# Normalised linear attention and a gated linear unit on one core: more buffers in four rings, and a new rotation of all of them, in an unchanged order

## The chip, the cores and the metric

The kernel runs on one core of a Trainium2 chip. The metric is the time of one execution on the device, in microseconds. PE is the matmul engine (TensorE), PEld its weight loads, DVE the vector engine, ACT the scalar engine, POOL is GpSimd, and SP the engine whose queue issues most DMAs. A name like L838 is line 838 of the kernel's file; the file has the same number of lines before and after the change, so a line number means the same in both.

## What is computed

Eight batches of eight heads, 576 positions, 64 values a head, in float32. The second half calls the first one's result `x`, with the heads side by side (512 columns).

```python
kv = np.einsum('bhsd,bhse->bhde', k, v)
out = np.einsum('bhsd,bhde->bhse', q, kv)
rms = np.sqrt(np.mean(out * out, axis=-1, keepdims=True) + 1e-06)
x = out / rms * g_norm            # then (B, H, S, D) -> (B, S, H*D)
...
for k in range(K):                # K = 5, a causal convolution along the positions
    gate_pre += conv_w[k][None, None, :] * xp[:, k:k + S, :]
gate = 1.0 / (1.0 + np.exp(-gate_pre))
val = x @ w_val
return (gate * val @ w_out).astype(np.float32)
```

The inputs `moe_w_val`, `moe_conv_w` and `moe_w_out` are of type float64; the kernel narrows them itself.

## The kernel before

**A list of steps.** The whole program is one string, `PLAN`, of 1242 steps in the order in which they are issued. Each step names a small function and its arguments (batch, chunk or column block, part), and after an `@` the buffers that its new data go to. An engine executes its own instructions strictly in the order of the list; between engines, and between an instruction and a DMA, a step waits by semaphores for whatever wrote its inputs, and for whatever last read or wrote the buffer that it takes. These waits follow from the list's order and from the buffers named in it. A PSUM bank counts as one buffer, even where a step uses half of it.

**Buffers.** `ROOMS` (L275) says how many buffers there are of each kind and how long one is; `new` (L283) hands out the one that the plan names:

```python
ROOMS = {"w64": (3, 1024), "ot": (3, 512), "wexp": (2, 512), "gate": (3, 576), "xs": (4, 576), "x": (2,
         512), "qT": (2, 2304), "k0": (1, 1152), "k1": (1, 1152), "v0": (1, 1152), "v1": (1, 1152), "ss": (2,
         36), "rt": (2, 36), "sq": (2, 520)}
...
rooms["bank"] = [psum.tile([P, 512], FP32, name=f"bank{n}") for n in range(8)]
...
room = rooms[tag][picked.pop(0)]
```

**The steps of a batch, in the order of the data.**
- `load_half`, `load_q` (L348, L358): DMAs of k, v and q from SP's queue. `turn_q` (L500, L503): DVE transposes q.
- `kv_product` (L476): PE makes k'v in two banks, 64 x 64 at a time; `kv_copy` (L490): ACT copies it out.
- `raw_pair`, `raw_tail` (L551): PE multiplies q by it, two chunks of 128 positions (or the last 64) into two banks. `square` (L600): ACT squares them into an `sq` buffer; `sums` (L607): DVE adds up; `powers` (L617): POOL takes the power -1/2; `normalise` (L636): ACT scales the raw product into an `x` buffer.
- `turn_blocks` (L661): DVE transposes `x` in blocks of 32; `move_blocks` (L669): DMAs from SP's and POOL's queues bring the blocks to their places in `xT`. The last chunk goes through PE instead (`turn_x`, L648; `keep_x`, L655). `halo` (L676): POOL.
- `gate_start` (L680): ACT begins a `gate` buffer; `gate_tap` (L686): DVE adds four taps; `gate_end` (L693): ACT's sigmoid.
- `x_sums` (L732), `val_fast` (L747), `val_keep` (L754 to L768): the product with `w_val` in seven half products instead of eight (Strassen's scheme), with sums of inputs made by DVE and sums of outputs put together by ACT copies and DVE adds. In a bank that goes on accumulating, the next half product waits until the copy in between has been taken. (`val_product`, L698, is the plain form for the first two batches.)
- `gated` (L711): DVE multiplies value and gate; this is the last reader of a `gate` buffer.
- `token_sums` (L816), `fast_product` (L838), `fast_keep` (L848 to L861): the product with `w_out`, two batches at a time, by the same scheme. `fast_product` uses one bank for `a`, and one bank for both `b` and `c`. `fast_keep` copies or adds into two `ot` buffers; `out_product` (L785) and `keep_out` (L793) do the last 64 positions plainly.
- `store` (L870): four DMAs of an `ot` buffer to the output, from SP's queue; `store_last`, from two queues, at the end.

At the start `narrow_weight` (L400 to L426) turns float64 weights into float32 with DVE and ACT; it takes `ot` and `wexp` buffers as scratch, and `start_warm` (L464) runs a few matmuls without use of their results.

The two functions that name the bank of half products and the copy of one half of it:

```python
elif bank != "a" and ("c", i, p) not in st:
    both = ps([P, 2, C // 2], f"cb{i}_{p}")
    st["b", i, p], st["c", i, p] = both[:, 0], both[:, 1]
...
elif n == 1:
    nc.scalar.copy(out=second[:, HIGH], in_=c)     # L852, fast_keep i p 1
```

Of the kernel before, what the change touches and what calls it, by code (L numbers as in the profile page):

```python
# [21 lines left out]
stage_weight cw 0 @ 0; turn_q_rows 0 1 @ 1; turn_q_rows 0 4 @ 0; sort_q 0 1 @ 0; turn_q_rows 0 0 @ 2;  # L22
sort_q 0 4; turn_q_rows 0 3 @ 3; turn_q_rows 0 2 @ 4; sort_q 0 0; start_warm 3 256 @ 0; load_q_rows 1 1;
load_q_rows 1 0; narrow_weight cw 0 0 @ 0; narrow_weight cw 0 5 @ 0; narrow_weight cw 0 1; sort_q 0 2;
stage_weight wval 3; kv_product 0 0 @ 1 2; narrow_weight cw 0 2; load_half k 1 0; narrow_weight cw 0 3;
load_half v 1 0; start_warm 1 256 @ 0; narrow_weight cw 0 6 @ 1; narrow_weight cw 0 4; kv_half 0 0;
narrow_weight cw 0 7; sort_q 0 3; turn_cw @ 4; kv_product 0 1; keep_cw; load_half k 1 1; stage_weight wval 2;
raw_half 0 3 0 @ 3; narrow_weight wval 1 5 @ 1; kv_half 0 1; load_half v 1 1; narrow_weight wval 1 0 @ 0;
raw_half 0 2 0 @ 4; narrow_weight wval 1 6 @ 0; narrow_weight wval 1 1; raw_half 0 3 1;
narrow_weight wval 0 5 @ 2; raw_half 0 2 1; stage_weight wout 1 @ 0; square 0 3 @ 0;  # L30
narrow_weight wval 0 6 @ 1; raw_half 0 4 0 @ 1; narrow_weight wval 1 2; sums 0 3 @ 0 0; raw_half 0 4 1;
square 0 2 @ 1; raw_half 0 0 0 @ 2; narrow_weight wval 0 0 @ 1; stage_weight wout 0 @ 1; powers 0 3;
square 0 4 @ 0; raw_half 0 0 1; sums 0 2; narrow_weight wval 1 3; raw_half 0 1 0 @ 0; sums 0 4; square 0 0 @ 1;
raw_half 0 1 1; narrow_weight wval 1 4; turn_q_rows 1 2 @ 5; load_q 2 2; square 0 1 @ 0; sums 0 0; powers 0 2;
narrow_weight wval 0 1; narrow_weight wval 1 7; turn_q_rows 1 0 @ 6; narrow_weight wval 0 2; sums 0 1;
turn_q_rows 1 3 @ 7; sort_q 1 2 @ 0; normalise 0 3 @ 0; narrow_weight wval 0 3; narrow_weight wval 3 5 @ 0;
turn_x 0 3 @ 5; powers 0 1; narrow_weight wval 3 6 @ 2; sort_q 1 0; turn_q_rows 1 1 @ 3; sort_q 1 3;
narrow_weight wval 3 0 @ 0; normalise 0 2 @ 0; narrow_weight wval 3 1; turn_q_rows 1 4 @ 7; normalise 0 4 @ 1;
turn_x 0 2 @ 4; keep_x 0 3; narrow_weight wval 0 4; narrow_weight wval 3 2; turn_x 0 4 @ 1;
kv_product 1 0 @ 6 5; narrow_weight wval 0 7; keep_x 0 4; narrow_weight wval 3 3; normalise 0 1 @ 1; halo 0;  # L40
keep_x 0 2; normalise 0 0 @ 0; stage_weight wout 2 @ 2; turn_x 0 1 @ 1; narrow_weight wval 3 4; turn_x 0 0 @ 2;
keep_x 0 1; narrow_weight wval 2 5 @ 1; val_product 0 1 1 @ 4; load_half k 2 0 @ 0; keep_x 0 0;
narrow_weight wval 3 7; narrow_weight wval 2 0 @ 1; gate_start 0 1 @ 0; narrow_weight wval 2 6 @ 2;
load_half v 2 1 @ 0; gate_start 0 0 @ 1; gate_tap 0 1 3; kv_product 1 1; gate_start 0 3 @ 2; gate_tap 0 0 3;
load_q 2 0; sort_q 1 1; val_product 0 3 1 @ 2; gate_tap 0 3 3; sort_q 1 4; kv_copy 1 0; kv_copy 1 1;
narrow_weight wval 2 1; narrow_weight wout 1 0 @ 0; narrow_weight wout 1 5 @ 1; gate_tap 0 0 2;
narrow_weight wval 2 2; raw_tail 1 @ 6 5; gate_tap 0 3 2; narrow_weight wval 2 3; raw_pair 1 3 @ 7 3;
square 1 4 @ 0; narrow_weight wout 1 6 @ 0; narrow_weight wout 1 1; val_product 0 1 0 @ 1; sums 1 4 @ 0 0;
square 1 3 @ 1; narrow_weight wval 2 4; powers 1 4; load_half v 2 0 @ 0; narrow_weight wout 1 2;
gate_tap 0 0 1; load_q 2 1; narrow_weight wout 1 3; sums 1 3; val_product 0 0 1 @ 0; keep_val 0 3 1;  # L50
narrow_weight wval 2 7; powers 1 3; square 1 2 @ 1; narrow_weight wout 1 4; normalise 1 4 @ 0; sums 1 2;
val_product 0 0 0 @ 2; val_sums 0; powers 1 2; normalise 1 3 @ 1; gate_tap 0 3 1; gate_tap 0 0 0;
val_product 0 2 0 @ 5; gate_tap 0 1 2; gate_end 0 0; gate_tap 0 3 0; keep_val 0 1 1; keep_val 0 0 0;
keep_val 0 0 1; narrow_weight wout 0 0 @ 1; raw_pair 1 1 @ 4 6; keep_val 0 1 0; narrow_weight wout 1 7;
narrow_weight wout 0 1; gated 0 0; turn_x 1 3 @ 1; square 1 0 @ 1; gate_tap 0 1 1; turn_x 1 4 @ 0;
val_product 0 2 1 @ 2; normalise 1 2 @ 1; sums 1 0; turn_q 2 0 @ 0; powers 1 0; gate_start 0 2 @ 1;
narrow_weight wout 0 5 @ 0; turn_x 1 2 @ 3; load_q 2 3; narrow_weight wout 2 5 @ 2; square 1 1 @ 1;
val_product 0 3 0 @ 7; narrow_weight wout 2 0 @ 0; gate_tap 0 2 3; keep_x 1 4; keep_x 1 3; keep_x 1 2;
gate_tap 0 2 2; load_half k 2 1 @ 0; narrow_weight wout 0 2; stage_weight wout 3 @ 0; kv_product 2 0 @ 3 1;
gate_tap 0 2 1; narrow_weight wout 0 3; sums 1 1; keep_val 0 2 0; val_product 1 0 1 @ 0; keep_val 0 3 0;  # L60
narrow_weight wout 0 4; keep_val 0 2 1; powers 1 1; gate_end 0 3; narrow_weight wout 0 6 @ 1;
normalise 1 0 @ 1; gate_tap 0 1 0; val_product 1 1 1 @ 2; narrow_weight wout 2 6 @ 0; halo 1; turn_q 2 2;
normalise 1 1 @ 0; narrow_weight wout 0 7; kv_product 2 1; gate_tap 0 2 0; keep_val 1 0 1; gate_end 0 1;
val_sums 1; turn_x 1 0 @ 0; gate_end 0 2; turn_q 2 1; turn_x 1 1 @ 4; keep_x 1 0; val_product 1 3 1 @ 6;
gated 0 3; load_q 3 0; narrow_weight wout 2 1; gated 0 2; kv_copy 2 1; keep_x 1 1; turn_q 2 3;
gate_start 1 1 @ 2; val_product 1 1 0 @ 4; load_q 3 1; weight_sums 0; kv_copy 2 0; keep_val 1 1 1; val_sums 2;
narrow_weight wout 2 2; gate_tap 1 1 3; keep_val 1 3 1; narrow_weight wout 2 3; raw_pair 2 3 @ 2 3;
load_half v 3 0 @ 0; narrow_weight wout 3 0 @ 1; load_half v 3 1 @ 0; narrow_weight wout 3 5 @ 1;
gate_tap 1 1 2; raw_pair 2 1 @ 1 6; square 2 2 @ 1; gated 0 1; square 2 3 @ 0; val_product 1 0 0 @ 0;
# [5 lines left out]
normalise 2 2 @ 1; sums 2 1; token_sums 0 0 2 @ 2; powers 2 1; square 2 0 @ 1; turn_blocks 2 3;
fast_product 0 0 0 @ 0; load_half k 3 1 @ 0; gate_start 1 3 @ 1; turn_q 3 1; fast_product 0 1 0 @ 2;
fast_keep 0 0 0 @ 0; weight_sums 1; keep_val 1 2 0; normalise 2 1 @ 0; fast_product 0 0 1 @ 3; sums 2 0;
gate_tap 1 0 3; raw_tail 2 @ 5 4; powers 2 0; fast_product 0 0 2; fast_keep 0 0 1 @ 2; weight_sums 2;
token_sums 0 0 3; fast_product 0 0 3; fast_keep 0 0 2; square 2 4 @ 1; turn_blocks 2 2; keep_val 1 2 1;
fast_product 0 0 5; fast_keep 0 1 0 @ 1; turn_blocks 2 1; normalise 2 0 @ 1; fast_product 0 0 4; sums 2 4;  # L80
fast_keep 0 0 5; powers 2 4; fast_product 0 1 2; gate_tap 1 0 2; store 0 0; kv_product 3 0 @ 6 1;
turn_blocks 2 0; fast_keep 0 1 2; normalise 2 4 @ 0; fast_keep 0 0 4; move_blocks 2 0; turn_q 3 2;
fast_product 0 1 4; gate_tap 1 0 1; move_blocks 2 2; turn_x 2 4 @ 4; fast_product 0 1 1 @ 5; gate_tap 1 0 0;
keep_x 2 4; move_blocks 2 1; kv_product 3 1; weight_sums 3; turn_q 3 3; move_blocks 2 3; fast_product 0 0 6;
gate_tap 1 3 3; kv_copy 3 0; kv_copy 3 1; gate_end 1 0; load_half v 4 0 @ 0; raw_pair 3 3 @ 1 6; load_q 4 0;
gate_tap 1 3 2; fast_keep 0 1 1 @ 0; gated 1 0; raw_pair 3 1 @ 3 4; fast_keep 0 1 4; square 3 3 @ 1;
gate_tap 1 1 1; fast_keep 0 0 6; fast_product 0 1 3; sums 3 3 @ 0 1; square 3 1 @ 0; load_half k 4 0 @ 0;
# [143 lines left out]
def kernel(  # L231
# [683 lines left out]
```

## Time and profile before

| | |
|---|---|
| time, median of 3 runs | 306.85 us (304.8 to 308.93) |
| the profiled execution | 305.46 us |
| its span, first to last instruction | 303.6 us |
| mean granted clock of PE | 0.995 |
| instructions | 8765 |

The span is what the profile's times refer to; 1.86 us lie around it. The page of the profile gives each engine's busy time, views by window give it by stage, and the timeline gives each instruction with the idle time of its engine ahead of it and what ended that time. PE's rows come in pairs for a float32 matmul of the program: "x4" at L838 is one half product of two matmuls.

### The profile page before, as it was taken

The numbers are of one execution on the slowest core, as the hardware profiler recorded it, in microseconds if no ns is written. First come the engines' busy times: TensorE is split into PE (matmuls) and PEld (weight loads), VectorE is DVE, ScalarE is ACT, GpSimd is POOL, SyncE is SP. The second block draws the span as 40 slices with busy tenths as digits, with TensorE's granted clock in tenths as the row PEclk, the third lists the DMA queues.
The fourth block names the chain that finished last, engine by engine and source line by source line (L and its number), as shares of the span: only waits on it lengthen the run. The fifth ranks groups of instructions, "written<-read, shape, count | busy, mean of one in ns | idle before, by whom it ended". The sixth has DMA issues, their size and how long they took to land.

```text
span 303.6 us, 8765 instructions
## 1 busy us (share of the span) xinstructions
PE 292.6 (96%) x3333; PEld 226.0 (74%) x3333; DVE 273.0 (90%) x482; ACT 194.5 (64%) x606; POOL 112.5 (37%) x127
## 2 busy tenths in 40 slices
PE   7989999999999989999999999999999999999993
PEld 3778777788786765877878757787877588788582
DVE  1899999999998999999999999999999999999612
ACT  2998989989567654983586537682878354434220
POOL 3072355045647046165327552245635731000000
PEclk9999999999999999999999999999999999999997
DMA  7999976578479466978688587928411721112423
GB/s 270 378 385 367 302 189 215 146 231 250 122 190 333 123 186 143 316 200 241 177 238 284 135 220 192 328 53 225 104 37 42 169 69 35 37 43 63 104 69 104
DMA packets 32073, 55.51 MB, mean 183 GB/s; under 512 B 6166, under 2 KB 14358, under 8 KB 32032
## 3 DMA queue, kind: packets, MB, share of 16 engines
q1 hardware_dynamic: 29520, 49.76, 55.8%
q0 software_dynamic: 1632, 3.17, 4.4%
q10 hardware_dynamic: 880, 2.03, 1.9%
q8 instruction: 26, 0.43, 0.6%
q14 instruction: 15, 0.12, 0.1%
HBM read 39.21 MB, written 9.44 MB: 160 GB/s over the span
## 4 chain that ended last, share of the span: by engine, by line
PE 70%; DMA 12%; DVE 9%; SPq 4%; issue 2%; ACT 1%; DVEq 0%; ACTq 0%
PE bank L838 29%; PE bank L747 23%; DMA qs<-in_q_dram 9%; PE bank L785 5%; PE bank L698 4%; PE bank L551 4%; DVE gate L686 3%; PE bank L476 3%; DMA k<-in_k_dram 2%; SPq L669 2%; DMA out_dram<-ot 2%; PE bank L648 1%; SPq L358 1%; PE bank L521 1%; PE bank L515 1%
## 5 line engine op out<-in xcount | busy, mean ns | idle before, releaser
L617 POOL TENSOR_TENSOR rt<-ss,mhalf 128x8 f32<-128x8 f32 (+3 forms) x38 | 68.0, 1794 | 100.3 <-DVE ss L607 100.3
L686 DVE SCALAR_TENSOR_TENSOR gate<-xT,cwT,gate 128x576 f32<-128x576 f32 x128 | 101.7, 812 | 2.3 <-ACT gate L680 0.8
L636 ACT ACTIVATE x<-bank,rt 128x64 f32<-128x64 f32 x252 | 55.8, 359 | 6.3 <-POOL rt L617 4.1
L838 PE MATMUL bank<-wsum,w 128*128 128x256 f32 x192 | 48.9, 385 | 0.9 <-ACT ot L850 0.6
L838 PEld LDWEIGHTS bank<-wsum,w 128*128 128x128 f32 x192 | 35.4, 190 | 8.8 <-DVE w L816 1.1
L747 PE MATMUL bank<-xs,vsum 128*128 128x288 f32 x144 | 38.1, 408 | 0.0
L669 POOL DMA_DIRECT2D xT<-y x48 | 26.4, 557 | 27.2 <-ACT ot L852 13.7
L838 PE MATMUL bank<-wout,gv 128*128 128x256 f32 x128 | 33.0, 384 | 0.3 <-ACT x L636 0.3
L698 PE MATMUL bank<-xT,wval 128*128 128x288 f32 x128 | 32.8, 409 | 0.0
L747 PEld LDWEIGHTS bank<-xs,vsum 128*128 128x128 f32 x144 | 27.1, 190 | 7.4 <-ACT x L636 0.4
L693 ACT ACTIVATE gate<-gate 128x576 f32<-128x576 f32 x32 | 22.2, 704 | 10.8 <-DVE gate L686 10.6
L848 DVE TENSOR_TENSOR ot<-bank,ot 128x512 f32<-128x512 f32 (+1 forms) x32 | 17.5, 547 | 12.4 <-PE bank L838 7.1
L698 PEld LDWEIGHTS bank<-xT,wval 128*128 128x128 f32 x128 | 23.7, 190 | 6.1
L600 ACT ACTIVATE sq<-bank 128x256 f32<-128x256 f32 (+1 forms) x70 | 21.9, 390 | 9.0 <-PE bank L551 8.6
L747 PE MATMUL bank<-xT,wval 128*128 128x288 f32 x96 | 26.8, 411 | 0.5 <-DMA out_dram<-ot 0.2
L838 PEld LDWEIGHTS bank<-wout,gv 128*128 128x128 f32 x128 | 23.8, 190 | 4.4 <-ACT x L636 0.5
L680 ACT ACTIVATE gate<-xT,cwT 128x576 f32<-128x576 f32 x32 | 25.0, 807 | 3.1 <-DVE gv L711 3.1
L607 DVE TENSOR_REDUCE ss<-sq 128x8 f32<-128x520 f32 (+1 forms) x40 | 24.9, 632 | 0.7 <-ACT sq L600 0.6
L711 DVE TENSOR_TENSOR gv<-gv,gate 128x576 f32<-128x576 f32 x32 | 23.6, 751 | 1.0 <-ACT gate L693 0.8
L747 PEld LDWEIGHTS bank<-xT,wval 128*128 128x128 f32 x96 | 17.7, 190 | 5.0 <-issue 0.7
L551 PEld LDWEIGHTS bank<-kv,qT 64*64 64x64 f32 x1008 | 16.4, 134 | 5.6 <-issue 2.4
L676 POOL COPY xT<-xT 128x124 f32<-128x124 f32 x32 | 16.0, 538 | 10.5 <-ACT xT L655 10.5
(93 smaller groups left out, 451.5 us busy)
## 6 DMA issues: line engine op xcount, KB each, us to landing
qs<-in_q_dram SPq DMA_DIRECT2D x96, 140.0 KB, 4.0
out_dram<-ot SPq DMA_DIRECT2D x140, 64.0 KB, 1.7
k<-in_k_dram SPq DMA_DIRECT2D x14, 576.0 KB, 6.0
v<-in_v_dram SPq DMA_DIRECT2D x12, 576.0 KB, 5.5
xT<-y SPq DMA_DIRECT2D x48, 64.0 KB, 2.9
xT<-y POOLq DMA_DIRECT2D x48, 64.0 KB, 3.2
y<-in_moe_w_val_dram SPq DMA_DIRECT2D x4, 512.0 KB, 11.6
w<-in_moe_w_out_dram SPq DMA_DIRECT2D x4, 512.0 KB, 10.0
```

The source lines that it names most:

```text
L551: nc.tensor.matmul(st["raw", b, c][r][cols, to * D:(to + 1) * D], st["qT", b][rows, hp, first:first + D], kvs[b % 2][rows, hp, :], start=T ...
L607: nc.vector.reduce_sum(out=st["ss", b][:, FIRST[c]:FIRST[c] + n], in_=st["sq", b, c][:, 0:n], axis=AX.X)
L617: nc.gpsimd.tensor_tensor(out=st["rt", b][:, which], in0=st["ss", b][:, which], in1=mhalf[:, which], op=ALU.pow)
L636: nc.scalar.activation(out=x[:, to * D:(to + 1) * D], in_=raw[:, h * D:(h + 1) * D], func=AF.Copy, scale=root[:, to:to + 1])
L669: (nc.sync if i % 2 else nc.gpsimd).dma_start(out=xTs[b % 2][i * TB:(i + 1) * TB, :, first:first + P], in_=y[a * TB:(a + 1) * TB, i])
L680: nc.scalar.activation(out=gate[:], in_=xTs[b % 2][:, jt, HALO:SX], func=AF.Copy, scale=cwT[:, K - 1, jt:jt + 1])
L686: nc.vector.scalar_tensor_tensor(out=gate[:], in0=xTs[b % 2][:, jt, tap * TB:tap * TB + S], scalar=cwT[:, tap, jt:jt + 1], in1=gate[:], op ...
L693: nc.scalar.activation(out=gate[:], in_=gate[:], func=AF.Sigmoid)
L698: nc.tensor.matmul(val[:], wval[:, kc, jt * P:(jt + 1) * P], xTs[b % 2][:, kc, HALO + n * SV:HALO + (n + 1) * SV], start=(kc == 0), stop=( ...
L711: nc.vector.tensor_tensor(out=both, in0=both, in1=st["gate", b, jt][:], op=ALU.mult)
L747: nc.tensor.matmul(st[bank, "val", b, mj][:], weights_[:, k], tokens()[:, k], start=(n in (0, 1, 3) and k == 0), stop=(k == NK // 2 - 1), ...
L838: nc.tensor.matmul(st[bank, i, p], tokens()[:, k], weights_[:, k], start=(n < 2 and k == 0), stop=(k == NK // 2 - 1), skip_group_check=True)
```

## The change

Four rings get one buffer more each: output buffers (`ot`) 3 to 4, gates 3 to 4, x chunks 2 to 3, buffers of squares 2 to 3. The number of PSUM banks stays at 8. In the plan, each step that takes a buffer now takes the one that has been free longest, in the enlarged rings as in the others and in the banks.

Each engine's and each DMA queue's instructions stand in the same order as before, one by one; the only new instruction is one memset of 128 x 8 (L325) for the third buffer of squares. The list interleaves the engines a little differently, which matters only where two steps of different engines share a buffer.

How far apart the takings of one buffer lie, counted in takings of its kind, from the two plans:

| kind | before: buffers, least, mean | after: buffers, least, mean |
|---|---|---|
| `ot` | 3, 1, 2.96 | 4, 2, 4.00 |
| `gate` | 3, 1, 3.00 | 4, 2, 4.00 |
| `x` | 2, 1, 1.95 | 3, 2, 2.97 |
| `sq` | 2, 1, 1.97 | 3, 2, 3.00 |
| `xs` | 4, 1, 3.45 | 4, 3, 4.00 |
| bank | 8, 1, 7.55 | 8, 1, 7.92 |

The diff, with a few of the plan's 209 lines:

```diff
-    ROOMS = {"w64": (3, 1024), "ot": (3, 512), "wexp": (2, 512), "gate": (3, 576), "xs": (4, 576), "x": (2,
+    ROOMS = {"w64": (3, 1024), "ot": (4, 512), "wexp": (2, 512), "gate": (4, 576), "xs": (4, 576), "x": (3,
              512), "qT": (2, 2304), "k0": (1, 1152), "k1": (1, 1152), "v0": (1, 1152), "v1": (1, 1152), "ss": (2,
-             36), "rt": (2, 36), "sq": (2, 520)}
+             36), "rt": (2, 36), "sq": (3, 520)}
...
-val_keep 2 0 2; gate_end 1 3; val_fast 2 1 1 @ 7; val_keep 2 1 2; gate_start 1 2 @ 2; val_fast 2 0 4;
+val_keep 2 1 2; gate_start 1 2 @ 0; load_q 4 1; val_fast 2 0 4; sums 3 0; val_keep 2 0 1; gated 1 1;
...
-kv_product 4 1; token_sums 0 1 0 @ 2; token_sums 0 1 2 @ 1; fast_keep 0 2 0 @ 1; raw_tail 3 @ 3 1;
+fast_keep 0 2 0 @ 2; load_q 4 2; raw_tail 3 @ 0 3; token_sums 0 1 2 @ 2; fast_product 0 3 0 @ 2;
...
-fast_product 2 2 1 @ 3; gate_tap 6 1 2; gated 6 2; val_fast 6 1 3 @ 0; val_keep 6 1 4; gate_start 6 0 @ 2;
-val_keep 6 1 5; fast_product 2 2 3; val_keep 6 1 3; normalise 7 4 @ 0; gate_tap 6 1 1; val_fast 7 1 0 @ 1;
-fast_keep 2 2 1 @ 0; token_sums 2 1 1; turn_x 7 4 @ 2; val_fast 7 1 3 @ 7; val_keep 7 1 0; token_sums 2 1 3;
+gate_tap 6 1 2; fast_product 2 2 1 @ 4; gate_start 6 0 @ 1; gated 6 2; val_fast 6 1 3 @ 5; normalise 7 4 @ 2;
+val_keep 6 1 4; fast_keep 2 2 1 @ 2; val_keep 6 1 5; fast_product 2 2 3; val_keep 6 1 3; gate_tap 6 1 1;
+val_fast 7 1 0 @ 2; token_sums 2 1 1; turn_x 7 4 @ 3; token_sums 2 1 3; val_keep 7 1 0; val_fast 7 1 3 @ 6;
```

More of the change, by code (lines that the diff above doesn't have):

```diff
@@ L75 @@
[L75 to L84, printed above, removed]
@@ new lines @@
+powers 2 2; keep_val 1 3 0; normalise 2 3 @ 1; narrow_weight wout 3 7; narrow_weight wout 2 4;
+load_half k 3 0 @ 0; load_q 3 2; val_product 1 2 0 @ 7; normalise 2 2 @ 0; narrow_weight wout 2 7; sums 2 1;
+token_sums 0 0 2 @ 1; powers 2 1; square 2 0 @ 2; fast_product 0 0 0 @ 5; turn_blocks 2 3; gate_start 1 3 @ 3;
+load_half k 3 1 @ 0; turn_q 3 1; fast_product 0 1 0 @ 1; fast_keep 0 0 0 @ 2; keep_val 1 2 0; weight_sums 1;
+normalise 2 1 @ 2; fast_product 0 0 1 @ 0; sums 2 0; raw_tail 2 @ 7 3; gate_tap 1 0 3; powers 2 0;
@@ new lines @@
+turn_blocks 3 1; fast_product 0 2 3; sums 3 4; move_blocks 3 1; fast_product 0 3 2; fast_keep 0 2 4;
+gate_tap 2 1 3; val_fast 2 0 3 @ 1; powers 3 4; move_blocks 3 3; fast_keep 0 3 2; turn_q 4 2; move_blocks 3 2;
+fast_product 0 3 1 @ 4; gate_tap 2 0 2; normalise 3 4 @ 2; move_blocks 3 0; fast_product 0 2 5; gate_tap 2 0 1;
+gate_start 2 3 @ 3; turn_q 4 3; fast_product 0 2 6; gate_tap 2 0 0; raw_pair 4 3 @ 0 6; gate_tap 2 1 2;
+out_product 0 8 @ 3; square 4 3 @ 0; fast_keep 0 2 5; fast_keep 0 2 6; gate_tap 2 3 3; store 0 4;
@@ new lines @@
+square 4 2 @ 1; gate_end 2 0; sums 4 3 @ 0 0; gate_tap 2 1 1; powers 4 3; gate_tap 2 3 2; load_half v 5 0 @ 0;
+turn_x 3 4 @ 5; sums 4 2; store 0 5; keep_x 3 4; gate_tap 2 1 0; powers 4 2; val_keep 2 0 3; gate_end 2 1;
+val_fast 3 0 0 @ 7; x_sums 3 0 @ 1; fast_keep 0 3 1 @ 1; normalise 4 3 @ 1; x_sums 3 1 @ 0; raw_pair 4 1 @ 1 5;
+load_half v 5 1 @ 0; gated 2 1; load_q 5 0; fast_product 0 3 3; val_keep 3 0 0; x_sums 3 3 @ 3;
+normalise 4 2 @ 0; turn_blocks 4 3; fast_product 0 3 4; gated 2 0; load_half k 5 0 @ 0; gate_start 2 2 @ 0;
@@ new lines @@
+val_fast 3 0 2; fast_keep 0 3 4; gate_tap 2 3 1; gate_start 3 2 @ 1; fast_product 0 3 5; square 4 1 @ 2;
+gate_tap 2 3 0; square 4 0 @ 0; val_fast 3 1 1 @ 0; turn_blocks 4 2; fast_keep 0 3 5; val_fast 3 1 0 @ 6;
+x_sums 3 2 @ 2; store 0 6; fast_product 0 3 6; val_keep 3 1 0; sums 4 0; gate_end 2 3; sums 4 1;
+val_fast 3 1 2; gated 2 3; load_q 5 1; powers 4 1; val_fast 3 0 1 @ 4; val_keep 3 1 2; gate_tap 2 2 3;
+val_keep 3 1 1; val_keep 3 0 2; val_fast 3 1 4; fast_keep 0 3 6; gate_tap 2 2 2; keep_out 0 8 @ 2; powers 4 0;
@@ new lines @@
+gated 2 2; kv_copy 5 1; val_fast 3 0 3 @ 0; fast_keep 1 0 0 @ 0; square 4 4 @ 1; token_sums 1 0 0 @ 0;
+kv_copy 5 0; store 0 7; move_blocks 4 0; token_sums 1 0 1; fast_product 1 0 1 @ 7; move_blocks 4 1;
+gate_tap 3 0 3; fast_product 1 0 2; move_blocks 4 3; gate_tap 3 0 2; val_fast 3 1 3 @ 3; fast_keep 1 0 2;
+sums 4 4; gate_start 3 3 @ 3; val_keep 3 1 4; powers 4 4; fast_keep 1 0 1 @ 3; gate_tap 3 0 1; val_fast 3 1 6;
+token_sums 1 0 3; normalise 4 4 @ 0; fast_product 1 0 4; turn_q 5 3; fast_product 1 0 3; turn_q 5 2;
@@ new lines @@
+powers 6 1; gate_start 5 2 @ 3; turn_blocks 6 2; fast_product 2 1 2; token_sums 2 0 3; fast_keep 2 0 2;
+square 6 0 @ 0; gate_tap 5 2 3; fast_product 2 0 5; fast_keep 2 1 2; normalise 6 1 @ 1; sums 6 0;
+fast_product 1 2 0 @ 1; token_sums 1 1 0 @ 1; powers 6 0; fast_product 2 0 4; fast_keep 2 0 5; turn_blocks 6 3;
+store 2 0; fast_product 2 1 4; fast_keep 2 0 4; normalise 6 0 @ 0; turn_q 7 0 @ 1; fast_product 2 1 1 @ 6;
+gate_tap 5 2 2; fast_product 2 0 6; load_q 7 3; turn_blocks 6 1; raw_tail 6 @ 2 7; fast_keep 2 0 6;
@@ new lines @@
+val_fast 6 1 2; halo 6; fast_keep 1 3 4; normalise 7 0 @ 2; gate_tap 5 1 0; fast_product 1 3 6; x_sums 6 2 @ 2;
+val_keep 6 1 2; val_fast 6 0 2; gated 5 0; sums 7 1; val_fast 6 1 1 @ 6; val_keep 6 0 2; turn_blocks 7 0;
+gate_end 5 1; powers 7 1; val_fast 6 1 4; turn_blocks 7 2; val_keep 6 0 1; fast_keep 1 3 6; val_keep 6 1 1;
+fast_keep 1 3 5; store 1 7; gate_end 5 3; val_fast 6 0 4; normalise 7 1 @ 1; gated 5 3; val_fast 6 1 5;
+gated 5 1; store 1 6; val_fast 6 0 3 @ 4; gate_start 6 3 @ 3; token_sums 2 1 2 @ 0; turn_blocks 7 1;
@@ L212 @@
 gate_tap 7 1 0; store 3 1; fast_product 2 3 5; gated 7 0; gate_end 7 1; fast_product 3 1 0 @ 3;
[L213 to L214 removed]
+fast_keep 2 3 5; gate_start 7 3 @ 3; gate_tap 7 2 2; val_fast 7 1 5; store 2 6; fast_keep 3 1 0 @ 1;
+fast_keep 2 3 4; val_fast 7 1 6; val_keep 7 1 5; gate_tap 7 3 3; fast_product 3 1 3; val_keep 7 1 6;
```

337 lines of the change are left out of this document (155 added, 182 removed).

## The prediction

> **What bounds the kernel now.** I read the page's busy times first, then the same by stage, then the chain of waits and the timeline of each engine where a stage shows a hole.
>
> ```profile
> PE 292.6 (96%) x3333; PEld 226.0 (74%) x3333; DVE 273.0 (90%) x482; ACT 194.5 (64%) x606; POOL 112.5 (37%) x127
> ```
>
> PE is the bound, and DVE is close behind. By stage (after the times come PE, PEld, DVE, ACT, POOL busy, the granted clock, the DMA share and GB/s):
>
> ```profile
> 94.00:111.00 17.00, 15.25 (x211) 11.65 (x210) 15.27 (x29) 11.10 (x40) 3.00 (x4) 1.00 0.69 213
> 111.00:264.00 153.00, 152.45 (x1585) 116.43 (x1584) 149.43 (x249) 94.66 (x313) 68.75 (x81) 1.00 0.59 163
> 264.00:287.00 23.00, 22.95 (x103) 16.94 (x101) 21.36 (x34) 8.81 (x20) 0.00 (x0) 1.00 0.26 66
> 300.00:303.60 3.60, 0.00 (x0) 0.00 (x0) 0.00 (x0) 0.00 (x0) 0.00 (x0) 0.58 0.35 93
> ```
>
> After the first 20 us, PE idles 1.75 us in one stage of 17 us and less than 0.6 us in each of the others up to 287; DVE idles 1.73 us there and 3.57 us from 111 to 264. A busy PE is not a PE at its peak, so I also need the step of its stream when nothing holds it. The chain gives it:
>
> ```profile
> 126.13 0.86 PE bank L838 x4
> 127.00 1.94 PE bank L747 x8
> ```
>
> Four instructions of an output product (L838) take 0.865 us, four of a value product (L747) 0.97. Against these steps I look for starts that come late. The one cluster is this, PE first, then ACT, then DVE (start, length, what, in brackets the idle time before it and its releaser):
>
> ```profile
> 96.64 2.21 PE L747 MATMUL bank<-xT,vsum 128*128 128x288 f32 x8 [0.65 <-ACT gv L758]
> 105.83 1.13 PE L838 MATMUL bank<-wout,gv 128*128 128x256 f32 x4 [0.34 <-ACT x L636]
> 107.56 1.13 PE L838 MATMUL bank<-wsum,w 128*128 128x256 f32 x4 [0.60 <-ACT ot L850]
> 108.85 1.99 PE L838 MATMUL bank<-wsum,w 128*128 128x256 f32 x8 [0.16 <-ACT gv L768]
> ```
>
> ```profile
> 95.53 0.77 ACT L680 ACTIVATE gate<-xT,cwT 128x576 f32<-128x576 f32 x1 [1.78 <-DVE gv L711]
> 99.37 1.75 ACT L636 ACTIVATE x<-bank,rt 128x64 f32<-128x64 f32 x8 [0.84 <-DVE y L661]
> 104.03 1.74 ACT L636 ACTIVATE x<-bank,rt 128x64 f32<-128x64 f32 x8 [0.33 <-DVE y L661]
> 107.13 0.37 ACT L850 COPY ot<-bank 128x256 f32<-128x256 f32 x1 [1.36 <-DMA out_dram<-ot]
> ```
>
> ```profile
> 96.34 1.67 DVE L686 SCALAR_TENSOR_TENSOR gate<-xT,cwT,gate 128x576 f32<-128x576 f32 x2 [0.84 <-ACT gate L680]
> 98.57 0.71 DVE L661 STREAM_TRANSPOSE y<-x 128x512 f32<-128x512 f32 x1 [0.19 <-ACT x L636]
> 106.06 0.68 DVE L816 TENSOR_TENSOR w<-w,gv 128x512 f32<-128x512 f32 x1
> 110.94 0.42 DVE L848 TENSOR_TENSOR ot<-bank,ot 128x256 f32<-128x256 f32 x1 [0.62 <-ACT gv L768]
> ```
>
> All four waits of ACT are waits for a buffer: a gate that is still multiplied (L711), an x chunk not yet transposed (L661, twice), an output buffer not yet stored. PE's late starts stand behind them: its releaser each time is a copy that was queued on ACT.
>
> **The change, part by part.** Every engine and every DMA queue issues the same instructions in the same order; only the buffers differ, and so the waits. One set-up memset is new; the two like it take 65 ns each, and DVE then idles 5.5 us for the first inputs: cost 0.
>
> *The cluster, 94 to 111.* With a fourth gate, gate_start runs when ACT is free, at 93.37 + 0.38 = 93.75 instead of 95.53, and the copy that frees PE (L758, next in the queue) ends near 94.8 instead of 96.59. PE's previous group starts at 94.86 and lasts 0.97, so PE starts at 95.83 instead of 96.64: 0.81. The third x chunk takes away 0.84 and 0.33, the fourth output buffer 1.36. PE's start at 105.83 could have been at 105.01 + 0.27 = 105.28 (16 small products of the group at 105.01): 0.55. The one at 107.56 could follow at 105.83 + 0.865 + 0.10 = 106.80 (after each wait the second step is 0.10 late, hence 1.13 above where four undisturbed take 1.03): 0.76. The one at 108.85, at 107.56 + 0.97 = 108.53: 0.32. Sum 2.44. But the product at 107.56 also needs DVE's sum, which ends at 106.06 + 0.68 = 106.74. DVE gains 0.84 + 0.19 = 1.03 by then, so it is there at 105.71 and PE cannot start before 105.76: 1.80 gained, not 2.12. With the 0.32 behind it, PE leads by **2.1 us** at 111 (bounds: 0.8 if only the gate matters, 2.44 if DVE holds nothing). DVE, whose 0.62 at 110.94 was a wait for PE, leads by 1.65.
>
> *From 111 to 264.* PE has 0.55 us idle left, so its lead can hardly grow: 0 (to 0.45, two starts at 181 and 222). DVE's lead grows by part of its 3.57 us: its waits for PE (0.52 and 0.21) by what PE leads beyond it, some 0.45, and a little of those for ACT; I take 0.6 of bounds 0 and 3.57, nearer the bottom since most of its idle time is the pipeline's own, under 0.15 us a time. DVE's lead is then 2.2. The other ACT waits that go in this stage (for stores 1.23 at 211.86; for gates 0.94 at 244.78) lie before copies for which PE does not wait.
>
> *One wait is new and late.* I laid the new buffers over the old times: 92 waits of PE are new, and 91 of them end before PE's old start or within 0.1 us of it. The other:
>
> ```profile
> 246.42 0.37 ACT L852 COPY ot<-bank 128x256 f32<-128x256 f32 x1
> 245.35 1.03 PE L838 MATMUL bank<-wout,gv 128*128 128x256 f32 x4
> ```
>
> The list now has the copy of half a bank (fast_keep 2 2 1) ahead of the product into its other half (fast_product 2 2 3); it was behind. So PE waits for ACT at 245.35. ACT no longer waits 0.94 for its gate there, so the copy starts at 245.48 and ends at 245.85: PE starts 0.55 late, and 0.10 for the next step. PE also loses what it leads beyond ACT, which follows DVE: 2.1 - 1.65 = 0.45. Cost **1.1** (bounds: 0 if ACT is well ahead; 246.79 - 245.35 = 1.44, + 0.16 = 1.6 beyond any lead if it isn't). Behind the waiting product stand value products and, through them, DVE's adds; DVE has other work in its queue.
>
> *From 264 on.* PE's starts at 263.35, 281.55 and 287.05 wait for DVE sums and adds and are 0.26, 0.31 and 0.20 late; DVE's lead of 2.2 covers them: **0.8** gained (0 if DVE gained nothing). ACT's store waits (0.84, 0.72) hide under a PE that is 22.95 of 23.00 us busy. The end (the last copy at 298.58, its four stores, 3.6 us without matmuls) is the same.
>
> *Before 94.* The waits that go here (for squares, x, narrowed weights) are on ACT and DVE, 0.2 to 0.3 us each; PE's late starts there are the first inputs, and 0.36 for a load of k. I take 0, up to 0.5.
>
> Sum: 2.1 - 1.1 + 0.8 = **1.8 us**. The profiled execution took 305.46 us (span 303.6, 1.86 around it), so 303.7; the median of the runs shown, 306.85, lies 1.39 above it, and on that footing I forecast **305.0 us**, 0.6% less. A measurement here can tell about 2% (6.1 us; the three runs spread over 4.1) from no change.
>
> One rule bears on how much could be open. The Trainium skill, "Perfetto Trace Analysis", section "Identifying the Most-Contended Engine", says to judge TensorE by the busy share of weight loads, not of matmuls. By it 74% counts, a quarter of the span is open, and a gap that recurs can mean too few buffers (section "Optimization Strategy"). Here a load takes 190 ns of a 216 ns step even in an unbroken stream, so 88% is its most in L838; the sum above does not use the rule, and D below is what it would make.
>
> **Rivals.**
> *B, no gain* (306.9): DVE, 97% busy from 20 to 264, is the true bound and its order is kept; PE's lead of 2.1 is spent in waits for DVE sums. For it: 107.56 is already held by DVE. Against: DVE's own 1.65 us in the cluster were waits, and they go.
> *C, slower* (308.5): the shared bank at 245. ACT is not early, PE loses 1.6 there, and nothing of the cluster stays, as DVE holds PE elsewhere: 305.46 + 1.6, + 1.39 for the median. It decides from the point where ACT's copy comes later than 245.3. Over 2% it would need four such places, and I find one.
> *D, much faster* (294): all of the weight loads' waits after 20 us that name an engine or a DMA are buffer waits. They add up to 12.8 us (longest 1.1): 306.85 - 12.8. Against: most are 0.3 to 0.4 us at changes of tile size and end under the matmuls still running.
> *E, slower by a clock* (319): rotating through more banks leaves PE short pauses, and the clock falls. The last stage above has 0.58 granted after 1.4 us without matmuls began it; a stage of 17 us at 0.58 would take 17/0.58 = 29.3, so 12.3 more. Against: 1.00 in every stage with work, the cluster's 1.75 us of idle included. The Trainium skill, "TensorE: Matmul & The Clock Gate", section "A second HAM failure mode: psum-queue depth-cycling", speaks for it: cycling through PSUM banks idled the PE often enough for its clock to swing. By that rule the cluster should show it before, and it doesn't.
> *The change does nothing*: excluded, as the late starts name buffers that become more.
>
> **How the numbers follow.** Forecast 0.68, B 0.13, C 0.09, D 0.07, E 0.03. The range is 301.5 to 308.2: from a gain of 4 us or so (every late start after 20 us, at a low run) to C with a run at its middle, with 1.5 us for the spread of the runs; it leaves out D, E and the ends. Over 2% faster is D, 0.07; over 2% slower E and 0.02 of C, 0.05; 0.88 between.
>
> **What would show it.** Right: PE's starts of the cluster undelayed, ACT without waits for L711, L661 or stores there, PE's idle from 94 to 111 below 0.5 us, a new wait of 0.4 to 1.5 us of PE for ACT's L852 near 243, and PE waits for L816 and L848 gone after 260. Wrong: new PE waits for ACT of over 1 us at more than one place, DVE idle unchanged at 5 us from 94 to 264, a clock under 1.00 before 300, or a span below 298 or above 306.

## The result, and the profile after

| | before | after |
|---|---|---|
| median time | 305.82 us (304.4 to 308.93, 21 runs) | 302.94 us (301.69 to 305.54, 21 runs) |
| ratio | | 0.9906 (95%: 0.988 to 0.9932) |
| the profiled execution, its span | 305.46, 303.6 us | 305.54, 303.8 us |

The change makes the kernel 2.9 us (0.94%) faster; forecast were 1.8 us and 305.0. The time lies in the range, and the direction is clear of the noise though the gain is small. The forecast stood on the median of three runs, 306.85; the median of 21 is 1.03 us lower, and that is half of the 2.06 us by which the time came out below 305.0. The other half is the gain, which was larger than forecast. The profiled execution happens to be the slowest of the 21 after the change, so its span must not be compared with the one before. It has to be read by stage; a second and a third profile of the same kernel (below) have spans of 301.6 and 300.2.

The busy times of the page are nearly those of before, with POOL's 5.0 us larger:

```profile
PE 290.7 (96%) x3333; PEld 225.8 (74%) x3333; DVE 272.6 (90%) x483; ACT 193.2 (64%) x606; POOL 117.5 (39%) x127
```

By stage, with the columns of the prediction's table:

```profile
20.00:94.00 74.00, 71.10 (x1152) 57.37 (x1149) 70.98 (x124) 61.74 (x187) 38.77 (x32) 1.00 0.78 223
94.00:111.00 17.00, 16.78 (x221) 13.56 (x220) 16.89 (x30) 13.02 (x48) 5.26 (x6) 1.00 0.84 253
111.00:264.00 153.00, 151.58 (x1583) 116.22 (x1582) 149.50 (x250) 93.57 (x312) 69.50 (x81) 1.00 0.61 164
264.00:287.00 23.00, 22.96 (x103) 17.57 (x104) 21.57 (x35) 9.08 (x21) 0.00 (x0) 1.00 0.24 61
300.00:303.80 3.80, 0.00 (x0) 0.00 (x0) 0.00 (x0) 0.00 (x0) 0.00 (x0) 0.78 0.47 132
```

From 94 to 111 PE idles 17.00 - 16.78 = 0.22 us where it idled 1.75, DVE 0.11 where it idled 1.73 (in this execution the same work comes 2.7 us later, so the two windows do not hold quite the same instructions; the table of stretches below does not have this fault). The new idle time is in the first row: 2.9 us of PE's 74. Here is its largest piece, in the timeline of POOL, ACT and PE:

```profile
37.46 10.79 POOL L617 TENSOR_TENSOR rt<-ss,mhalf 128x8 f32<-128x8 f32 x3 [0.55 <-DVE ss L607]
46.83 1.74 ACT L636 ACTIVATE x<-bank,rt 128x64 f32<-128x64 f32 x8 [1.99 <-POOL rt L617]
48.63 0.66 PE L648 MATMUL bank<-ident,x 128*128 128x128 f32 x4 [1.86 <-ACT x L636]
```

and the same place of POOL before the change:

```profile
36.80 4.61 POOL L617 TENSOR_TENSOR rt<-ss,mhalf 128x8 f32<-128x8 f32 x2 [0.55 <-DVE ss L607]
45.19 1.64 POOL L617 TENSOR_TENSOR rt<-ss,mhalf 128x8 f32<-128x8 f32 x1 [3.78 <-DVE ss L607]
```

In this one execution the second of the three powers, at 40.1, took 6.69 us where it took 1.96, and ACT and PE stood behind it. PE reaches the cluster at 96.62 instead of 93.89. In the cluster itself the waits have gone. PE first, then ACT:

```profile
106.90 1.13 PE L838 MATMUL bank<-wout,gv 128*128 128x256 f32 x4
108.25 2.83 PE L838 MATMUL bank<-wsum,w 128*128 128x256 f32 x12 [0.22 <-DVE w L816]
110.92 1.03 PE L838 MATMUL bank<-wout,gv 128*128 128x256 f32 x4
96.23 0.78 ACT L680 ACTIVATE gate<-xT,cwT 128x576 f32<-128x576 f32 x1
97.48 3.40 ACT L636 ACTIVATE x<-bank,rt 128x64 f32<-128x64 f32 x16
104.96 1.73 ACT L636 ACTIVATE x<-bank,rt 128x64 f32<-128x64 f32 x8
106.53 0.42 ACT L850 COPY ot<-bank 128x256 f32<-128x256 f32 x1
```

None of the four ACT rows has a wait: not the gate (1.78 before), not the two x chunks (0.84 and 0.33), not the output buffer (1.36). Of the three products at L838 that began late, the one of 105.83 now starts without a wait (106.90), and the other two are part of an unbroken 12; what is left is one wait for DVE's sum (0.22). And the new wait at 245 is there, one place, as the prediction laid it out (PE's weight load names the releaser):

```profile
245.84 0.39 ACT L852 COPY ot<-bank 128x256 f32<-128x256 f32 x1
246.28 0.73 PEld L838 LDWEIGHTS bank<-wout,gv 128*128 128x128 f32 x4 [0.57 <-ACT ot L852]
246.28 1.13 PE L838 MATMUL bank<-wout,gv 128*128 128x256 f32 x4
```

Since matmul number n is the same one in every profile, PE's lead over the profile of before can be taken at any mark. A stretch between two marks is free of what came earlier. This is where PE gained and lost in the three profiles of the changed kernel, in us (marks by the times of before):

| from, to | forecast | first | second | third |
|---|---|---|---|---|
| start to 93.9 | 0 | -2.73 | -0.71 | +0.62 |
| 93.9 to 112.4, the cluster | +2.1 | +2.50 | +2.50 | +2.40 |
| 112.4 to 244.4 | 0 | -0.41 | -0.29 | -0.08 |
| 244.4 to 246.2, the new wait | -1.1 | -0.39 | -0.38 | -0.39 |
| 246.2 to 297.7 | +0.8 | +0.38 | +0.37 | +0.37 |
| 297.7 to the end | 0 | +0.54 | +0.52 | +0.56 |

The last five rows add up to 2.6 to 2.9 us, which is the gain in the medians; the first row differs from run to run. All of this is measured against the one profile that was taken of the kernel before.

### The profile page after: what moved, and what is told of

Same layout as the page of the kernel before. It is cut to its first block, busy times and chain, and to the rows that moved or that the text cites. A ratio compares the mean times of both kernels' runs of the same rounds, so it can differ in the third digit from the quotient of the medians.

```text
span 303.8 us, 8763 instructions
## 1 busy us (share of the span) xinstructions
PE 290.7 (96%) x3333; PEld 225.8 (74%) x3333; DVE 272.6 (90%) x483; ACT 193.2 (64%) x606; POOL 117.5 (39%) x127
## 4 chain that ended last, share of the span: by engine, by line
PE 64%; DVE 15%; DMA 8%; SPq 4%; POOL 3%; issue 2%; ACT 2%; DVEq 0%
PE bank L838 29%; PE bank L747 19%; PE bank L698 6%; DMA y<-in_moe_w_val_dram 4%; PE bank L551 4%; DVE gate L686 4%; PE bank L476 4%; POOL rt L617 3%; PE bank L785 2%; DMA k<-in_k_dram 2%; DVE xs L732 2%; DMA out_dram<-ot 2%; DVE ss L607 2%; SPq L669 1%; ACT x L636 1%
## 5 line engine op out<-in xcount | busy, mean ns | idle before, releaser
L617 POOL TENSOR_TENSOR rt<-ss,mhalf 128x8 f32<-128x8 f32 (+3 forms) x38 | 72.6, 1923 | 98.2 <-DVE ss L607 97.0
L686 DVE SCALAR_TENSOR_TENSOR gate<-xT,cwT,gate 128x576 f32<-128x576 f32 x128 | 101.8, 813 | 2.8 <-ACT gate L680 1.8
L838 PE MATMUL bank<-wsum,w 128*128 128x256 f32 x192 | 48.3, 383 | 0.2 <-DVE w L816 0.2
L838 PEld LDWEIGHTS bank<-wsum,w 128*128 128x128 f32 x192 | 35.8, 190 | 7.0 <-issue 0.8
L838 PE MATMUL bank<-wout,gv 128*128 128x256 f32 x128 | 33.2, 386 | 0.1
L838 PEld LDWEIGHTS bank<-wout,gv 128*128 128x128 f32 x128 | 23.7, 190 | 4.6 <-ACT ot L852 0.6
L676 POOL COPY xT<-xT 128x124 f32<-128x124 f32 x32 | 16.3, 549 | 9.9 <-ACT xT L655 9.9
```

The costliest lines, as they stand in the source:

```text
L617: nc.gpsimd.tensor_tensor(out=st["rt", b][:, which], in0=st["ss", b][:, which], in1=mhalf[:, which], op=ALU.pow)
L686: nc.vector.scalar_tensor_tensor(out=gate[:], in0=xTs[b % 2][:, jt, tap * TB:tap * TB + S], scalar=cwT[:, tap, jt:jt + 1], in1=gate[:], op ...
L838: nc.tensor.matmul(st[bank, i, p], tokens()[:, k], weights_[:, k], start=(n < 2 and k == 0), stop=(k == NK // 2 - 1), skip_group_check=True)
```

## The experiments

Theory: PE's starts in the cluster were late for want of a gate, an x chunk and an output buffer; a copy ahead of a product in a shared bank costs a little at 245; the rest follows. Rivals: the new rotation of the banks makes the difference; one ring alone does it; the gain is given back to DVE. Each ratio is to the kernel before on the same chip.

**The changed kernel again, for what repeats.** Twice, with nothing edited.

> The changed kernel once more. In its first profile, whose execution was its slowest (305.54 us against a median of 302.94), one power on GpSimd took 6.69 us at 40.1 instead of 1.96, and PE lost 2.0 us there; the stage of 17 us that the prediction looked at had gained 2.5. Theory (the gain is made in that stage, the loss is an accident of one execution): the PE stretch that takes 18.52 us before (from the start at 93.89 to that at 112.41) takes 16.0 to 16.2 again, no power is over 3 us or PE loses as much as it is longer, time 302 to 303.5. Rival (the long power belongs to the changed kernel): 6 to 7 us again at the third batch-1 power, PE 2 us late by 50.

> The changed kernel once more, as the measure for the other three: 302.3 to 302.9, ratio 0.990 to 0.992 of the kernel before, PE's wait of 0.39 us at 245 in place. If the second w_val part is narrowed at 15.2 us here, the early loss of 0.7 us is chance; at 16.6 a third time, it belongs to this list.

Measured: 302.67 us (ratio 0.9915, 0.9885 to 0.9945) and 302.25 (0.9904, 0.987 to 0.9938). The long power came in neither; the three powers there took 4.61 us for the first two and 1.69 for the third, in the third profile. The cluster, the wait at 245 and the end repeat within 0.1 us.

**Rings alone and banks alone.** The list of the kernel before, once with the four larger rings, once with the changed kernel's banks:

```diff
 # rings
-"ot": (3, 512) ... "gate": (3, 576) ... "x": (2, 512) ... "sq": (2, 520)
+"ot": (4, 512) ... "gate": (4, 576) ... "x": (3, 512) ... "sq": (3, 520)
 # banks, for one
-out_product 0 8 @ 2
+out_product 0 8 @ 3
```

> The list and the PSUM banks of before, with only the four larger rings (gates, x, output buffers, squares), each rotated as in the changed kernel. Theory (ring waits on ACT are the whole gain): the PE stretch of 18.52 us takes 16.0 to 16.3, the new PE wait near 245 is not there, time 0.8 to 1.2% under before. Rival (the banks' rotation brings it): the stretch stays over 17.5 and the time within 0.4% of before.

> The list and the rings of before, with only the PSUM banks of the changed kernel. Theory (ring waits): the stretch of 18.52 us stays within 0.4 us, time within 0.4% of before. Rival (banks): the stretch falls to under 17 and the time by 0.7% or more.

Measured: rings 303.09 us (0.9933, 0.9902 to 0.9964), banks 305.32 (0.9997, 0.9973 to 1.0021). The rings carry the gain (0.67%, at its middle less than the 0.8 to 1.2 expected, but the interval takes in the whole change's 0.94); PE's stretch is 16.19 us, as expected, and the wait at 245 is not there. The banks don't change the time. Yet in its one profile the kernel with new banks also gained 1.12 us in the cluster. I did not expect that, and come back to it below.

**The gate alone.**

```diff
-"gate": (3, 576)
+"gate": (4, 576)
 ...
-gate_start 1 2 @ 2
+gate_start 1 2 @ 0
```

> Before with a fourth gate alone, rotated as in the changed kernel. Theory, by the prediction's steps: ACT's wait of 1.78 us for the multiplied gate goes, PE gains 0.8 at its start at 96.64; the waits for x chunks and for the store stay, so the stretch of 18.52 us takes 17.2 to 17.8, PE still waits for ACT's copy L850 behind the store. Rival (the store alone sets the end of the stretch, as the chain of waits has it, 3.22 us of it through that store): 18.2 or more, since the product at 107.56 starts when the store lands.

Measured: 304.76 us (0.9986, 0.996 to 1.0012). PE's start at 96.64 came 0.81 us earlier relative to 93.89 (lead 0.20, then 1.01), the figure of the prediction to the hundredth. The gain then disappeared at one place:

```profile
184.55 0.59 ACT L793 COPY ot<-bank 128x512 f32<-128x512 f32 x1 [1.96 <-DMA out_dram<-ot]
185.19 3.18 PE L747 MATMUL bank<-xs,vsum 128*128 128x288 f32 x12 [1.22 <-ACT ot L793]
```

ACT's copy waited for the store of an output buffer, which had been issued at 179.8 and landed at 184.48; PE lost 1.1 us. So in this profile a store's landing set the pace here, with three output buffers, once PE was earlier. It does not always cost as much: in the other profiles with three output buffers in which PE is earlier, those with new banks, with x and squares, and with gate and x, L793 waits 0.75, 0.41 and 0.47 us at the same place.

**Gate and output buffer, output buffer alone, x and squares alone.** The same edits, ring by ring, on the list of the kernel before.

> The kernel before with two of the larger rings, the fourth gate and the fourth output buffer. Theory 1, the parts lean on each other: with the fourth gate alone PE led by 1.2 us at 112 and lost 1.1 of it at 185, where ACT's copy L793 waited 1.96 us for the store of an output buffer; with the fourth output buffer too this wait goes, so the lead of 1.2 to 1.6 us stays to 297, the last stores give another 0.5, span near 301.7, time 1.7 to 2.0 us below the kernel before (ratio 0.994). Theory 2, the lead of the gate is lost to DVE whatever the buffers: lead at 200 of 0.1 us again, time within 0.6 us of the kernel before (0.998 or more).

> The kernel before with the fourth output buffer alone. Theory 1: it takes the store wait of L850 at 107 away (1.36 of ACT, so PE's 0.6 at 107.56, less what DVE's sum holds, 0.3 to 0.6), leaves PE's start at 96.64 as late as before, and makes the last stores 0.5 us shorter: 0.5 to 1.1 us below the kernel before (ratio 0.997). Theory 2: the end has nothing to do with it: the span after PE's last start stays 5.9 us, as before and in the two runs without a fourth output buffer. On the early loss: if the fourth output buffer brings it, the second w_val part is narrowed (DVE L417) at 16.6 us; if x or the squares do, at 15.2.

> The kernel before with the third x chunk and the third buffer of squares alone. Theory 1: ACT's waits for L661 (0.84, 0.33) go and with them PE's late start at 105.83 (0.3 to 0.5); L711's and the store's stay, so the stretch of PE from 93.9 to 112.4 takes 17.9 to 18.2 us against 18.5 before and 16.0 in the changed kernel; the end stays 5.9; time 0 to 0.6 us below the kernel before. Theory 2, the x chunk matters as much as the gate: stretch 17.4 or less. On the early loss: DVE L417's second at 16.6 us if x or the squares bring it, at 15.2 if the output buffer does, and if both this run and the one with the fourth output buffer show 15.2, it is chance or the sum of the shifts.

| kernel | median us | ratio (95%) | stretch 93.9 to 112.4, us | after PE's start at 297.7, us |
|---|---|---|---|---|
| before | 305.01 | 1 | 18.52 | 5.92 |
| gate and `ot` | 302.59 | 0.9899 (0.9864 to 0.9934) | 16.18 | 5.35 |
| `ot` | 303.48 | 0.9944 (0.9916 to 0.9971) | 17.34 | 5.39 |
| `x` and `sq` | 304.16 | 0.9968 (0.9939 to 0.9997) | 17.36 | 5.87 |

Gate and output buffer together give what the whole change gives (theory 1), with no wait at L793. The output buffer alone is worth 0.56% and also shortens the end. Both gained more than expected (ratios of 0.994 and 0.997). The kernel with x and squares gained as much in the cluster as theory 2 said, but by a way neither theory had: ACT's copy L850 didn't wait for a store though this kernel has three output buffers, and PE then waited for DVE:

```profile
106.05 2.18 PE L838 MATMUL bank<-wsum,w 128*128 128x256 f32 x9 [0.36 <-DVE w L816]
```

**Gate and x, without the output buffer.** If the output buffer matters only at the end, this must be as good as gate and output buffer, less 0.5 us.

> The kernel before with the fourth gate and the third x chunk, still three output buffers. Theory 1: the cluster is open as with gate and output buffer (stretch from 93.9 to 112.4 of 16.2 to 16.5 us), but ACT's copy L793 near 182 waits again 0.4 to 2 us for a store, and the end stays 5.9 us: PE keeps between 1.2 and 2.3 us of lead, and the time is 0.5 to 1.5 us above the kernel with gate and fourth output buffer (302.6), 303.1 to 304.1. Theory 2, the fourth output buffer matters only at the end: no loss at 185, 0.5 us above it at most, 303.1 or less.

Measured: 305.41 us (0.9999, 0.9967 to 1.003). Stretch 17.42, end 6.01. Theory 2 falls; theory 1 had the mechanism but not the place, which is in the cluster:

```profile
106.03 0.37 ACT L850 COPY ot<-bank 128x256 f32<-128x256 f32 x1 [1.92 <-DMA out_dram<-ot]
106.46 1.13 PE L838 MATMUL bank<-wsum,w 128*128 128x256 f32 x4 [1.15 <-ACT ot L850]
```

ACT came earlier to the same store and waited longer for it (1.92 us instead of 1.36); L793 waited only 0.47. This also explains the kernel with new banks. The store in question is the last of the four DMAs of its buffer. Its issue and landing, from the trace's DMA records, against ACT's copy:

| kernel | output buffers | last store issued, landed | L850 starts | its wait |
|---|---|---|---|---|
| before | 3 | 103.81, 107.03 | 107.13 | 1.36 |
| gate | 3 | 102.36, 105.82 | 105.92 | 1.62 |
| gate and x | 3 | 103.24, 105.94 | 106.03 | 1.92 |
| banks | 3 | 102.13, 103.86 | 105.61 | none |
| x and squares | 3 | 101.46, 103.19 | 104.34 | none |
| `ot` | 4 | 103.15, 106.22 | 105.14 | none |
| gate and `ot` | 4 | 103.01, 106.30 | 104.28 | none |

With three output buffers the copy cannot start before that landing, and where the landing is late, PE loses about 1.1 us. With four it starts before the landing. Some of these stores took 1.7 us, others 2.7 to 3.5, and around a late landing there is a pause in which the DMA engines move almost nothing. The rates of the kernel before and of that with new banks, in 40 slices of 0.2 us from 100 to 108:

```profile
GB/s 45 22 22 22 0 134 314 186 298 144 174 123 225 103 154 164 92 215 72 205 82 154 164 144 215 41 90 179 224 190 10 22 22 0 224 112 358 247 291 359
```

```profile
GB/s 283 115 215 205 205 72 215 62 154 164 92 215 72 205 82 143 174 10 179 157 269 359 202 381 306 202 381 202 336 247 179 135 23 45 202 291 269 247 157 381
```

Before, the pause is at 106.0 to 106.8, with the store issued at 103.81 still under way. With new banks it is at 106.4 to 106.8, and the store had landed at 103.86, since SP issued it 1.68 us earlier.

The late landings share something that the same view shows. It also lists the DMA queues, and one of the kind "instruction" has one transfer from 100 to 108 of the kernel before (then its MB and its share):

```profile
q8 instruction: 1, 0.02, 0.9%
```

By the trace's DMA records it is 16384 bytes long and runs from 104.65 to 105.85. SP's instruction that issues a load at 104.76 lasts 1.46 us there, where the next takes 0.42. All but two of the stores' packets of 2 KB are through by 105.19, and the last two start at 105.84 and 106.06, behind that transfer; the landing follows at 107.03. Each of the fourteen profiles has such a transfer in this stretch, 0.88 to 1.46 us long. In the six with a late landing (before, gate, gate and x, `ot`, gate and `ot`, rings) it begins while packets of the store are still to come, and the last two or more of them start only as it ends (to 0.02 us). In the other eight the store's last packet has started by the time it begins, to 0.01 us, and the store lands in 1.7 to 1.8 us. So here a late landing is one on which a transfer of instructions falls. No run moved that transfer, and why the landing comes 0.75 us after the last packet is open, as is whether the new banks sent the store earlier; the unchanged median (0.9997) speaks for chance.

**The wait at 245 taken away in two ways.** In the changed kernel's list alone the product goes ahead of the copy again; and the changed kernel's buffers on the list of the kernel before, where it always was ahead (14 steps of `narrow_weight`, `sort_q` and `sums` keep the buffers of before):

```diff
 # order
-fast_keep 2 2 1 @ 2; val_keep 6 1 5; fast_product 2 2 3;
+fast_product 2 2 3; fast_keep 2 2 1 @ 2; val_keep 6 1 5;
```

> The changed kernel with one step moved in its list: the product fast_product 2 2 3 again ahead of the copy fast_keep 2 2 1 of the other half of its bank, buffers untouched. Theory 1: only the wait at 245 goes; PE's lead does not drop by 0.39 us there, the time is 0.4 us below the changed kernel. Theory 2: PE takes the wait a few products later, for ACT or DVE: lead at 264 and time as in the changed kernel.

> All buffers and banks of the changed kernel, but with the list of the kernel before, in which the product fast_product 2 2 3 stands ahead of the copy fast_keep 2 2 1 into whose bank it writes. Theory 1: PE's new wait at 245 (0.39 us in both profiles of the changed kernel) is gone and nothing else changes: lead at 246 of 1.5 to 2.0, at 264 of 1.9 to 2.3, span near 301, 0.4 us below the changed kernel (302.3). Theory 2: PE then waits for DVE there or at 263 in its place, and the time is that of the changed kernel (302.7).

> All buffers of the changed kernel on the list of the kernel before, once more, beside the changed kernel on the same chip. Theory 1, the wait at 245 is all that tells them apart: 0.4 us below the changed kernel (ratio 0.998 to 0.999 of it). Theory 2, the list of the kernel before is better elsewhere too: 0.8 us or more below. The second w_val part may be narrowed at 15.2 or at 16.6 us in either, if that is chance.

PE there in the third profile of the changed kernel, and then with the product moved:

```profile
241.45 1.13 PE L747 MATMUL bank<-xT,wval 128*128 128x288 f32 x4
242.70 1.13 PE L838 MATMUL bank<-wout,gv 128*128 128x256 f32 x4
243.67 1.13 PE L747 MATMUL bank<-xT,wval 128*128 128x288 f32 x4
```

```profile
243.13 1.13 PE L747 MATMUL bank<-xT,wval 128*128 128x288 f32 x4
244.10 1.03 PE L838 MATMUL bank<-wout,gv 128*128 128x256 f32 x4
244.96 1.13 PE L747 MATMUL bank<-xT,wval 128*128 128x288 f32 x4
```

The step into the product is 1.25 us with the wait and 0.97 without, and the step after it 0.97 against 0.86: 0.39 together. In both profiles on the old list the lead doesn't change here either. The time is less clear: 302.06 us with the product moved (0.9883, 0.9839 to 0.9926); 301.81 and 302.78 with the old list (0.9874, 0.984 to 0.9909, and 0.9904, 0.9868 to 0.9941), beside 302.25 for the changed kernel (the 301.81 was measured at another time than the other three). Of the 0.4 us expected, 0.2 came in one kernel, far inside the intervals, and in the other the sign isn't settled. So the wait is shown in the profiles, and that a version without it is faster than the changed kernel is not. The profile with the product moved lost 0.83 us at another place, in the middle of one k'v group at 171 where PE paused 0.72 for nothing that the profile shows: one run says little about 0.4 us.

## Why the prediction was right, and where its steps were off

*The cluster, 2.1.* Right in place and cause; 2.40 to 2.50 measured. The output buffer's part of it belongs to a late landing of the store, as the one profile of before has it; with an early one (new banks, x and squares) the same 1.12 us came with three buffers. The gate's term (0.81) came out exactly. The output buffer's two terms (0.76 and 0.32) were 1.18 by the run with `ot` alone. The x chunk's 0.55 is the term that gives nothing. It was also put too large: it lets the 16 small products before that start take 0.27 us, and with gate and x, where nothing holds the start, they take 0.39 (103.78 to 104.17). With gate and `ot` but two x chunks, PE waits 0.34 at its place and the stretch is 16.18. With three x chunks beside them DVE's sum L816 holds PE by up to 0.36 instead, and the stretch is 15.91 to 16.20. So DVE does cap the cluster, as the prediction said, but at the cost of the x chunk's term; 0.32 off the product at 107.56 was too much, and the sum without a cap, 2.44, would have been nearer.

*What the rings are worth.* The prediction put the four waits side by side and added them up. The runs show an order: the fourth output buffer alone gives 0.56%, and the gate without it, alone or with the x chunk, is lost at the next store (0.9986 and 0.9999). The x chunk and the squares without it come out at 0.9968 (0.9939 to 0.9997); in their one profile the store landed early, so what they are worth by themselves isn't settled.

*The wait at 245, -1.1.* The mechanism is right and was found at the one place. The size was off by the term for lost lead, 0.45, which did not occur: ACT kept up with PE and more. In the first profile PE is 0.65 late here, so the copy's end at 246.23 stands for 245.58 in the times of before, where the prediction had 245.85. That leaves 0.55 - 0.27 = 0.28, and the 0.10 of the next step: 0.38, as measured.

*From 264 on, +0.8.* The wait at 263.35 gave 0.37; those at 281.55 and 287.05 gave nothing. DVE's lead was sized well: in the third profile DVE's sum is 2.92 us earlier there, 2.3 without the early part, where 2.2 was forecast. What failed is that it "covers them". PE stood at 2.55 and could gain only up to DVE's 2.92, and from there both run in step, so the later waits stay. DVE's lead is no reserve: in all fourteen profiles its sums there are ahead by what PE's next start is ahead, to 0.02 us. Nor does the error at 245 make this one: kernels without a wait at 245 (rings, gate and `ot`, the product moved, the old list) gain the same 0.37 at 263. That the two errors nearly cancel, -0.3 forecast and -0.01 measured, is luck.

*The end, "the same".* Wrong: 0.5 us shorter in every kernel with four output buffers (5.35 to 5.39 us after PE's last mark), the same within 0.1 in the four edited ones without (5.86 to 6.03, before 5.92). What SP's queue waits for from 296 to the end, before and after:

```profile
SPq L870 <- DMA out_dram<-ot: 1.1, 1, 1.1
```

```profile
SPq L870 <- DMA out_dram<-ot: 0.6, 1, 0.6
```

A store of SP's waited for an earlier store to land, and this wait is halved. The trace shows that it is no wait for a buffer. Each of SP's stores waits for the semaphore that it will itself set on landing. Before, the last but one of SP's stores (issued at 300.34) sets semaphore 103, which the first of ACT's last stores sets too, landing at 300.27. With four output buffers ACT's store sets 104, so the last but one goes out without that wait and only SP's last store has to wait. All nine profiles with four output buffers show this and the earlier end, and none of the five with three. I had counted the buffer waits of PE, ACT and DVE, and not the semaphores of the stores.

*Before 94, 0.* The stage takes part in the variation from run to run. The second w_val load is there for DVE (L417) at 15.2 to 15.3 us in seven of the fourteen profiles and at 16.3 to 16.6 in the other seven; in these PE is 0.75 us later at 42, on average. The changed kernel shows both, and so does the kernel with its buffers on the old list, so it differs from one execution to the next. Whether a fourth output buffer makes the late one more frequent (six of nine profiles with it, one of five without) isn't settled.

*The rivals.* B (DVE takes it all) and C (the shared bank) fall with the table by stretch. D would need 12.8 us; PEld's share stayed at 74 to 75% and the gain was less than a quarter of that. The share of weight loads, by which the Trainium skill ("Perfetto Trace Analysis", "Identifying the Most-Contended Engine") judges TensorE, beside a share of peak arithmetic that was not worked out here, doesn't hold here as a measure of what is open, though too few buffers was the cause, as its section "Optimization Strategy" suggests for a gap that recurs. E falls for what was measured: with the banks rotated alone the granted clock is 1.00 in each stage from 20 to 287 and the median is unchanged; the swings that the Trainium skill describes ("TensorE: Matmul & The Clock Gate", section "A second HAM failure mode: psum-queue depth-cycling") don't occur in its profile or in those of the changed kernel. One of the twelve executions with the banks rotated alone took 428.93 us at a mean granted clock of 0.658, of which there is no trace; the other eleven, and all 59 of kernels that rotate the banks together with the rings, had 0.995 or more, so it stays unexplained.

Of the signs that were to show it, the idle 0.22 us of PE and the ACT rows without waits came as written, the new wait with 0.39 just under its 0.4 to 1.5, and PE's waits after 260 went only in part. The span of 303.8 alone would have said nothing.

## What to carry to other kernels

Price a buffer by the wait that comes next, not only by the wait that it removes: here the rings' waits lay behind one another, and the ring that ends in a DMA decided, as its release came 1.7 us after the issue in some profiles and about 3 in others. A copy moved ahead of a matmul in a list costs time only if both use one PSUM bank and the copy is late; laying the new waits over the old times found the one such place in 92. For changes below 1%, compare stretches between the same two instructions over several profiles: the spans of the changed kernel differ by 3.6 us, and its stretch of the cluster by 0.1.

## What the runs showed of the hardware that I had not expected

- A power on POOL of 128 x 8 elements took 6.69 us once, against 1.96 at the same place before, with the same DVE instructions beside it (L686, 0.85 us each there and 0.83 before). In the next two profiles of the same kernel it took 1.96 again. The Trainium skill, "SBUF — State Buffer", section "Who interferes with whom", says that a DVE instruction with two SBUF inputs contends with a GpSimd instruction that reads SBUF, and that the order of issue decides which one is blocked; both kinds are there, POOL's power and DVE's L686. But they are there in every profile, DVE lost next to nothing, and no run here shows that this was the cause.
- A store of 64 KB takes 1.7 us from issue to landing in some profiles and about 3 us at the same place in others. In all six late ones a 16 KB transfer on the "instruction" queue, 0.88 to 1.46 us long, begins while packets of the store are still to come, and the last of them start as it ends. Which of the two it was decided about 1.1 us of PE's time in the five profiles with three output buffers.
- Beside the same transfers the issuing takes longer: in the stretch above, SP's instruction that issues a load lasts 1.0 to 1.8 us beside one, and 0.36 to 0.43 otherwise.
- Two stores that set the same semaphore run one behind the other: at the end SP's last store but one waited 1.1 us for a store of ACT's to land, and the kernel ended 0.5 us earlier where these two set different ones.
